# Reordering the gates, copies and banks around four stages of a two-layer SSM and MLP gradient kernel

## The chip, the cores and the metric

The kernel runs on one core of one Trainium2 chip. TensorE multiplies matrices into PSUM (eight banks of 128 partitions by 512 float32 values here), VectorE and ScalarE read PSUM and work element by element, GpSimd does small work and issues DMAs from its own queue, and SyncE (SP) issues most other DMAs. Each engine runs its own list of instructions in order and waits for the others through semaphores. The metric is the device time of one execution in microseconds; several executions are timed, and their median counts. One further execution was profiled, and all rows of the trace come from it.

## What is computed

The reference runs four residual layers forward and then takes the gradient of everything (a vector-Jacobian product with `grad_out`):

```python
x = A_q
x = x + A(layernorm(x))     # H3: q * (long_conv(short_conv(k) * v) + ...)
x = x + B(layernorm(x))     # MLP: silu(h @ w1) @ w2
x = x + A(layernorm(x))     # the same weights again
x = x + B(layernorm(x))
```

There are 2048 rows of 448 channels; the MLP is 1792 wide. In A, `k` is convolved with a four-tap kernel, multiplied by `v`, and convolved with a kernel as long as the sequence through an FFT of length 4096. That result, Y, does not depend on x, so both A layers use the same Y, and `A(n) = n * Y`. The kernel returns the output and the gradients of q, k, v, the two convolution kernels, the skip vector, w1 and w2 (nine outputs; the gradient of w1 is output 7, that of w2 output 8).

## The kernel before, in words

**Prefix** (`_ssm_prefix`). The convolution as matrix products: a first FFT stage, a turn of 128x128 blocks, a second stage, the product of two spectra, and the inverse. `k_turn` transposes the long kernel, 128 channels at a time (16 TensorE transposes into one PSUM tile of two banks, then a copy of each half, one by VectorE and one by ScalarE, L406 and L116/L117). `k_stage1` multiplies the turned kernel by the FFT matrix (L420). All PSUM tiles of this part share one tag `A` with four buffers of two banks. `PRODUCTS` is an order written out by hand: `M` is the product of the spectra on VectorE (L573), `V` the second inverse stage on TensorE (L260, L261, function `_fft_inv_stage2_full`), `v` its copy out of PSUM by ScalarE (a) or VectorE (d). The list ends `... V9 v7a v9a`. The last inverse stage `ys()` (L604, copies L607) follows and needs all the copies.

**Main** (class `Main`, `run`). The rows are worked in four chunks c of 512 rows, four tiles of 128 rows each; L is 0 for the first pair of layers and 1 for the second. The steps of a chunk are generators, and `weave("OOLOOG...")` advances one of them per letter, which writes TensorE's order out by hand:
- `fwd0(c)`: layer norm of the input (`_ln`, statistics L309, the power on GpSimd L314, normalisation L317), then `gate` (L727 the product with Y as tile `a_t`, L728 the sum into `X`), then the statistics and the normalisation of the second layer norm, `n01`. `fwd0_end` holds the normalisation back until a sum of O has run. `fwd1` does the same for the second pair of layers. `x_load` fetches the input rows of a later chunk on SP's queue.
- `H` and, in chunk 0, `Hh` (halves of 256 rows): the pre-activations (`full` L681 and `rest` L685 into `ps_h`), SiLU by ScalarE (L816 in `Hh`, L833 in `H`), and a copy of the pre-activations into `Dall` (L116 ScalarE or L117 VectorE). `Hh` has four groups; those listed in `single` use two one-bank tiles of tag `po`, the others a two-bank tile of tag `mm`; those in `dv` are copied by VectorE.
- `O`: the second MLP product (L850, `ps_o`, tag `po`) and the sum into X on VectorE (L855). In the second pair of layers of chunks 1 to 3 the sums have high priority.
- `G`: the gradient of the activations (L681 and L685 into `ps_g`), copied into `ghT` (L116 or L117; `dv` names the pairs that VectorE copies) and multiplied by the slopes (L1013). `slope` is ScalarE's derivative of SiLU (L843).
- `N`: the gradient of the MLP input (L889) and the backward of layer norm and gate on VectorE (L905 to L917, L1063 to L1068).
- `T`, `transp_half`: turns of normalised rows on TensorE (L658, L669), copied to `nT`.

PSUM tags in this part: `mm` two buffers of two banks, `po` and `tr` two buffers of one bank each.

**Suffix** (`_ssm_suffix`, `Jobs`). The gradients of the convolution, with the weight gradients woven in as jobs (`ps_d` L1115, 16 row blocks each of two operands). `Jobs.last` makes the last 128 rows of w1's gradient in two halves of 224 columns; `flush` turns a finished block with TensorE (L1220) and stores it.

**What sets the order.** In the main part TensorE's order is the program's. VectorE, ScalarE, GpSimd and SP are ordered by a planner that walks the program with estimated durations and takes the earliest traced instruction that is ready, or one of high priority. `tc.issue_after(i)` puts the instructions of its block behind instruction i where they run on the same engine.

Of the kernel before, what the change touches and what calls it, by code (L numbers as in the profile page):

```python
# [254 lines left out]
def _fft_inv_stage2_full(k, pa, pb, ci, psum):  # L255
    nc = k.nc
    ga, gb = (G_IAF, G_IBF) if ci % 2 else (G_IA, G_IB)
    pv = psum.tile([P, 8, P], FP32, name="ps_v", **k.pt["v"])
    for i in range(8):
        nc.tensor.matmul(pv[:, i, :], lhsT=pa[:, i * P:(i + 1) * P], rhs=k.Gpre[:, ga, :], start=True, stop=False)  # L260
        nc.tensor.matmul(pv[:, i, :], lhsT=pb[:, i * P:(i + 1) * P], rhs=k.Gpre[:, gb, :], start=False, stop=True)  # L261
    return pv
# [80 lines left out]
def _ssm_prefix(k):  # L343
# [4 lines left out]
    with ExitStack() as es:  # L348
# [51 lines left out]
        def k_turn(lo, hi):  # L400
            n = hi - lo
            kview = ksb[lo // P][:n].rearrange("p (n1 n2) -> p n2 n1", n2=16)
            pt = psum.tile([P, 2, 1024], BF16, name="ps_kt", **a_)
            pv = pt[:, :, 0:8 * n].rearrange("p g (i d) -> p g i d", d=n)
            for i in range(16):
                nc.tensor.transpose(pv[:, i // 8, i % 8, :], kview[:, i, :], k.ident[:n, :n])  # L406
            for g, e in enumerate((nc.vector, nc.scalar)):
                last = _copy(nc, e, Kt[:, 8 * g:8 * g + 8, lo:hi], pv[:, g])
# [167 lines left out]
        def V(ci):  # L576
            pab = live["V", ci]
            live["v", ci] = _fft_inv_stage2_full(k, pab[:, 1], pab[:, 0], ci, psum)

        def v(ci, part, eng):  # L580
            _copy(nc, eng, B1[:, 8 * ci:8 * ci + 8, :].rearrange("p a b -> p (a b)"), live["v", ci][:].rearrange("p a b -> p (a b)"))
# [34 lines left out]
class Main:  # L616
# [101 lines left out]
    def a_fwd(self, c, si, src, n_g, groups):  # L718
        _ln(self.k, self.ch, c, src, si, n_g, groups)
        self.gate(c, src, n_g)  # L720

# [19 lines left out]
    def fwd0(self, c):  # L741
# [187 lines left out]
    def run(self, ys):  # L929
# [47 lines left out]
        hs = [self.Hh(0, 1, nT, aT, dT2, 0, (1, 3), (1,)), self.Hh(0, 1, nT, aT, dT2, 1)]  # L977
# [4 lines left out]
        self.transp_half(self.n1[1], nT, GBLK, 1)  # L982
# [3 lines left out]
        for c in range(4):  # L986
# [8 lines left out]
            if c < 2:  # L995
# [477 lines left out]
```

## Time and profile before

| | us |
|---|---|
| median of 3 executions | 688.93 (688.62 to 689.18) |
| the profiled execution, its own time | 687.9 |
| its span, first to last instruction | 686.1 |
| TensorE busy | 665.3 (97%) |
| VectorE busy | 482.2 (70%) |
| ScalarE busy | 429.7 (63%) |
| GpSimd busy | 104.6 (15%) |

The granted TensorE clock is 0.999 of full speed over the span. In a timeline row stand the start, the duration, the engine, the line, the operation, output and input, the shape and the count; a bracket gives how long the engine idled before it and what ended that. "Who waited for whom" rows give total time, number of times and the longest. In rows of stretches the columns are the length, then busy time and count of TensorE, its weight loads, VectorE, ScalarE and GpSimd, then the granted clock, the DMA engines' busy share and GB/s. The prefix runs to about 84 us, chunk 0 starts there, the backward steps of chunk 0 at 154, those of chunks 1 and 2 near 246 and 338, and the suffix ends the span. Matmul durations contain latency and overlap, so the pitch of matmuls is taken from rows of many.

### The profile page before, as it was taken

The page shows a single profiled execution, that of the slowest core. Times are in us where ns is not written, and L with a number is a line of the kernel's source. Part 1 is how long each engine was busy: PE and PEld are TensorE (multiplying, and loading weights), DVE is VectorE, ACT ScalarE, POOL GpSimd, SP SyncE. Part 2 cuts the span into 40 slices and gives each one's busy share as a digit, 9 for nine tenths or more (in the row PEclk, how much of TensorE's full clock was granted, in tenths as well). Part 3 has the DMA queues.
Part 4 walks back from the last instruction along what each step waited for, and adds up shares of the span by engine and source line. Part 5 has one row for each costly group of instructions (what it writes and reads, how often), then busy time and mean ns, then how long its engine had stood idle before and what let it go on. Part 6 is the DMA issues. An engine that isn't in the chain of part 4 may idle for free.

```text
span 686.1 us, 14467 instructions
## 1 busy us (share of the span) xinstructions
PE 665.3 (97%) x5844; PEld 362.3 (53%) x5879; DVE 482.2 (70%) x1133; ACT 429.7 (63%) x528; POOL 104.6 (15%) x177
## 2 busy tenths in 40 slices
PE   8989999999999899999899999999999999999997
PEld 6876755554444344444444444544555555555666
DVE  5779954677879858898588874843937554528992
ACT  5988987888758668678477685123634543653431
POOL 1047320110010100101001000010111211102311
PEclk9999999999999999999999999999999999999999
DMA  8999989499788767598776799859599988956981
GB/s 316 248 278 316 342 191 227 112 228 258 191 241 228 219 163 193 123 250 231 182 162 193 218 241 375 241 173 205 200 238 354 324 274 323 351 173 223 324 308 42
DMA packets 203956, 162.60 MB, mean 237 GB/s; under 512 B 153505, under 2 KB 184244, under 8 KB 203122
## 3 DMA queue, kind: packets, MB, share of 16 engines
q1 hardware_dynamic: 190806, 113.35, 61.7%
q0 software_dynamic: 11088, 39.84, 17.1%
q10 hardware_dynamic: 1996, 8.49, 3.8%
q8 instruction: 46, 0.75, 0.4%
q14 instruction: 20, 0.16, 0.1%
HBM read 66.05 MB, written 54.60 MB: 176 GB/s over the span
## 4 chain that ended last, share of the span: by engine, by line
PE 77%; DVE 11%; ACT 5%; DMA 3%; issue 2%; POOL 1%; DVEq 0%; POOLq 0%
PE ps_d L1115 25%; PE ps_n L889 11%; PE ps_o L850 9%; PE ps_g L681 9%; PE ps_h L681 7%; PE ps_v L272 2%; PE ps_g L685 2%; PE ps_h L685 2%; DMA spec_K<-KAB 2%; DVE ln_st L309 1%; ACT KAB L116 1%; DVE lb_v L1063 1%; DMA KAB<-KAB 1%; PE ps_gK L1398 1%; PE ps_y L604 1%
## 5 line engine op out<-in xcount | busy, mean ns | idle before, releaser
L1115 PEld LDWEIGHTS <-dstat 128*128 128x128 bf16 x928 | 87.1, 98 | 75.7 <-issue 4.0
L889 PE MATMUL ps_n<-w1T,ghT 128*128 128x448 bf16 x448 | 94.5, 353 | 0.0
L850 PE MATMUL ps_o<-w2sb,aT 128*128 128x448 bf16 x448 | 89.2, 353 | 1.8 <-DVE X L855 1.8
L116 ACT CAST ghT<-ps_g 128x1024 bf16<-128x1024 f32 (+1 forms) x54 | 48.3, 899 | 60.9 <-PE ps_g L685 46.8
L681 PE MATMUL ps_h<-nT,w1sb 128*128 128x512 bf16 (+1 forms) x410 | 83.0, 336 | 2.1 <-DVE Dall L117 0.8
L681 PE MATMUL ps_g<-nT,w2T 128*128 128x512 bf16 x317 | 77.9, 379 | 1.6 <-ACT Dall L116 0.4
L889 PEld LDWEIGHTS <-ghT 128*128 128x128 bf16 x448 | 42.4, 98 | 45.3 <-issue 4.7
L850 PEld LDWEIGHTS <-aT 128*128 128x128 bf16 x448 | 43.2, 98 | 41.8 <-issue 3.5
L681 PEld LDWEIGHTS <-w1sb 128*128 128x128 bf16 x420 | 39.1, 98 | 37.1 <-issue 8.2
L1063 DVE SCALAR_TENSOR_TENSOR lb_v<-lb_u,n 128x448 bf16<-128x448 bf16 x60 | 37.2, 621 | 27.6 <-ACT lb_u L905 27.2
L833 ACT ACTIVATE aT<-ps_h 128x1024 bf16<-128x1024 f32 (+1 forms) x48 | 44.2, 922 | 19.7 <-PE ps_h L681 11.5
L116 ACT CAST Dall<-ps_h 128x1024 bf16<-128x1024 f32 (+2 forms) x60 | 54.8, 913 | 0.0
L843 ACT ACTIVATE Dall<-Dall 128x1024 bf16<-128x1024 bf16 (+1 forms) x48 | 53.3, 1186 | 0.1
L681 PEld LDWEIGHTS <-w2T 128*128 128x128 bf16 x336 | 31.3, 98 | 40.9 <-issue 5.9
L314 POOL TENSOR_TENSOR rstd<-ln_ve,mhalf 128x2 f32<-128x2 f32 (+1 forms) x24 | 19.6, 818 | 183.7 <-DVE ln_ve L313 183.7
L1115 PE MATMUL ps_d<-X,dstat 128*128 128x448 bf16 x224 | 47.6, 353 | 0.0
L1115 PE MATMUL ps_d<-go,dstat 128*128 128x448 bf16 x224 | 47.2, 353 | 0.0
L1115 PE MATMUL ps_d<-n3m,dstat 128*128 128x448 bf16 (+1 forms) x240 | 47.0, 340 | 0.0
L1115 PE MATMUL ps_d<-n1m,dstat 128*128 128x448 bf16 (+1 forms) x240 | 46.5, 340 | 0.0
L116 ACT CAST A1g<-ps_v 128x1024 bf16<-128x1024 f32 x14 | 14.9, 1064 | 36.5 <-PE ps_v L272 36.5
L855 DVE TENSOR_TENSOR X<-X,ps_o 128x448 bf16<-128x448 bf16 x32 | 19.5, 611 | 18.4 <-PE ps_o L850 18.2
L905 ACT ACTIVATE lb_u<-ps_n,rstd 128x448 bf16<-128x448 f32 x32 | 20.5, 639 | 16.8 <-PE ps_n L889 13.0
(210 smaller groups left out, 1111.9 us busy)
## 6 DMA issues: line engine op xcount, KB each, us to landing
dstat<-a_d SPq DMA_DIRECT2D x28, 512.0 KB, 5.0
dstat<-g_d SPq DMA_DIRECT2D x28, 512.0 KB, 5.4
a_d<-turned SPq DMA_DIRECT2D x16, 512.0 KB, 3.0
g_d<-turned SPq DMA_DIRECT2D x16, 512.0 KB, 3.0
a_d<-turned SPq DMA_DIRECT2D x16, 384.0 KB, 2.7
g_d<-turned SPq DMA_DIRECT2D x16, 384.0 KB, 2.8
spec_K<-KAB POOLq DMA_DIRECT2D x7, 512.0 KB, 6.3
KAB<-KAB POOLq DMA_DIRECT2D x28, 128.0 KB, 5.1
```

The lines of the kernel that those rows point to most:

```text
L116: return nc.scalar.copy(out, in_)
L314: nc.gpsimd.tensor_tensor(out=r[:, lo:hi], in0=ve[:, lo:hi], in1=k.mhalf[:, lo:hi], op=ALU.pow)
L681: self.nc.tensor.matmul(ps, lhsT=w[:, b, ft * P:(ft + 1) * P], rhs=x[:, b], start=(start and b == 0), stop=(stop and b == bs[2]))
L685: self.nc.tensor.matmul(ps, lhsT=w[sl, b, ft * P:(ft + 1) * P], rhs=x[sl, b], start=start, stop=stop)
L833: self.last_silu = nc.scalar.activation(aT[hh][:, o:o + hi - lo, :], ps(lo, hi), ACT.Silu)
L843: self.nc.scalar.activation(dT[hh][:, o:o + n, :], dT[hh][:, o:o + n, :], ACT.Derivative_silu)
L850: nc.tensor.matmul(po[:, :D], lhsT=aT[ft // 7][:, ft % 7, tl * P:(tl + 1) * P], rhs=self.w2sb[:, ft, :], start=(ft == 0), stop=(ft == NF - 1))
L855: self.last_o = nc.vector.tensor_tensor(out=X[:, t, :], in0=X[:, t, :], in1=po[:, :D], op=ALU.add)
L889: nc.tensor.matmul(pns[tl][:, :D], lhsT=gh[h][:, ft % 7, tl * P:(tl + 1) * P], rhs=self.w1T[:, ft, :], start=(ft == 0), stop=(ft == NF - 1))
L905: nc.scalar.activation(u0[:], pn[:, :D], ACT.Identity, scale=k.rstd[2 * L + 1][:, t:t + 1], accum_out=cp[:, tl, 0:1])
L1063: nc.vector.scalar_tensor_tensor(out=v[:], in0=u0, scalar=-1.0 / D, in1=n_t, op0=ALU.mult, op1=ALU.mult, accum_out=cp[:, 1:2])
L1115: self.nc.tensor.matmul(ps[:, cols], lhsT=st[:, t, :], rhs=mov[:, t, cols], start=(first and t == 0), stop=(last and t == NT - 1))
```

## The change

Five edits.

1. `fwd0` for chunks 1 to 3 no longer runs the gates at once; they move to a first step of `fwd0_end`, with the statistics of the second layer norm. For c above 1 that step stands behind the last traced sum of O, which is that of the first output tile, since the weave has a letter L after `OO`. For the rows of chunk 1, prepared in chunk 0, the gates keep their place. `x_load` moves behind the gates. The normalisation is a second step (the second L).
2. `G` of the second pair of layers in chunks 1 and 2 has all its copies on ScalarE; before, pairs 1 and 4 were copied by VectorE. Chunk 3 is as it was.
3. In chunk 0, `Hh` of the first half takes the third group through single `po` banks instead of the second, VectorE copies the pre-activations of the second and third groups instead of the second and fourth, and the copy of the second half's turn goes to VectorE.
4. `k_turn` uses two one-bank tiles per turn, and the inverse product 9, the last of the list, two tiles of four blocks, whose copies go to ScalarE and VectorE.
5. `Jobs.last` makes the first 336 columns as one product and the last 112 columns already turned, with the roles of the two operands exchanged; VectorE copies them, and SP stores them.

```diff
-def _fft_inv_stage2_full(k, pa, pb, ci, psum):
+def _fft_inv_stage2_full(k, pa, pb, ci, psum, parts):
     ...
-    pv = psum.tile([P, 8, P], FP32, name="ps_v", **k.pt["v"])
+    n = 8 // parts
+    pvs = [psum.tile([P, n, P], FP32, name="ps_v", **k.pt["v"]) for _ in range(parts)]
     for i in range(8):
-        nc.tensor.matmul(pv[:, i, :], lhsT=pa[:, i * P:(i + 1) * P], ...)
+        pv = pvs[i // n]
+        nc.tensor.matmul(pv[:, i % n, :], lhsT=pa[:, i * P:(i + 1) * P], ...)
     ...
@@ k_turn
-            pt = psum.tile([P, 2, 1024], BF16, name="ps_kt", **a_)
-            pv = pt[:, :, 0:8 * n].rearrange("p g (i d) -> p g i d", d=n)
+            pv = []
+            for g in range(2):
+                pt = psum.tile([P, 1024], BF16, name="ps_kt", **a_)
+                pv.append(pt[:, 0:8 * n].rearrange("p (i d) -> p i d", d=n))
     ...
@@ V and v
-            live["v", ci] = _fft_inv_stage2_full(k, pab[:, 1], pab[:, 0], ci, psum)
+            live["v", ci] = _fft_inv_stage2_full(k, pab[:, 1], pab[:, 0], ci, psum, 2 if ci == 9 else 1)
 
         def v(ci, part, eng):
-            _copy(nc, eng, B1[:, 8 * ci:8 * ci + 8, :]..., live["v", ci][:]...)
+            pvs = live["v", ci]
+            n = 8 // len(pvs)
+            for e, i in zip((eng, nc.vector), range(len(pvs))):
+                _copy(nc, e, B1[:, 8 * ci + n * i:8 * ci + n * i + n, :]..., pvs[i][:]...)
@@ fwd0
-            self.a_fwd(c, 0, xc, n00, ((0, 4),))
+            _ln(k, self.ch, c, xc, 0, n00)
             self.n0[c] = (n00, n01)
-            norm = _ln_parts(k, self.ch, c, self.xs(c), 1, n01, ((0, 4),))
-            next(norm)
-            self.norm = self.fwd0_end(c, norm, n01)
+            self.norm = self.fwd0_end(c, xc, n00, n01)
     ...
-    def fwd0_end(self, c, norm, n01):
+    def fwd0_end(self, c, xc, n00, n01):
+        norm = _ln_parts(self.k, self.ch, c, self.xs(c), 1, n01, ((0, 4),))
+        with self.tc.issue_after(self.last_o.ins) if c > 1 else nullcontext():
+            self.gate(c, xc, n00)
+            next(norm)
+        if c < 3:
+            self.x_load(c + 1)
+        yield
         with self.tc.issue_after(self.last_o.ins):
-            next(norm, None)
+            next(norm)
@@ run
-        hs = [self.Hh(0, 0, nT, aT, dT1, 0, (1, 3), (1,)), self.Hh(0, 0, nT, aT, dT1, 1)]
+        hs = [self.Hh(0, 0, nT, aT, dT1, 0, (1, 2), (2,)), self.Hh(0, 0, nT, aT, dT1, 1)]
     ...
-            self.transp_half(self.n0[0][1], nT, GBLK, 1)
+            self.transp_half(self.n0[0][1], nT, GBLK, 1, nc.vector)
     ...
     # the same two edits for the second pair of layers of chunk 0
     ...
                 if c == 0:
                     next(self.norm)
-            if c < 2:
-                self.x_load(c + 2)
+                    next(self.norm)
     ...
-                g = self.G(gT, gh2, dv=(1, 4))
+                g = self.G(gT, gh2, dv=(1, 4) if c == 3 else ())
                 if c < 3:
-                    weave("OOLOOGOGOGOGGOGTG", O=o, G=g, L=self.norm, T=...)
+                    weave("OOLOOLGOGOGOGGOGTG", O=o, G=g, L=self.norm, T=...)
@@ Jobs.last
-        for h in range(2):
-            cols = slice(h * D // 2, (h + 1) * D // 2)
-            ps = self.bank(None)
-            for i in range(2):
-                for n, _ in enumerate(self.mms(ps, sts[i], movs[i](), 0, NT, i == 0, i == 1, cols)):
-                    if h + i == 1 and n == 2:
-                        self.flush()
+        cols = slice(0, 3 * DC)
+        ps = self.bank(None)
+        for i in range(2):
+            yield from self.mms(ps, sts[i], movs[i](), 0, NT, i == 0, i == 1, cols)
+        nc.scalar.copy(o[:, cols], ps[:, cols])
+        self.flush()
+        self.pend = (ft, o, 0, 3)
+        ps = self.bank(None)
+        for i in range(2):
+            for t in range(NT):
+                nc.tensor.matmul(ps[:DC, 0:P], lhsT=movs[i]()[:, t, 3 * DC:D], rhs=sts[i][:, t, :], ...)
+                if i == 1 and t == 3:
+                    self.flush()
+                if t % 8 == 7:
                     yield 1
-            nc.scalar.copy(o[:, cols], ps[:, cols])
-            if h == 0:
-                self.flush()
-            self.pend = (ft, o, 2 * h, 2 * h + 2)
+        o7 = k.do7[ft % 4]
+        nc.vector.tensor_copy(o7[:, 3], ps[:DC, 0:P])
+        out7v = k.outs[7].rearrange("(c p) f -> p c f", p=DC)
+        nc.sync.dma_start(out=out7v[:, 3, ft * P:(ft + 1) * P], in_=o7[:, 3])
```

More of the change, by code (lines that the diff above doesn't have):

```diff
@@ L252, in _fft_stage2_full @@
     return ps
[L255 removed]
+def _fft_inv_stage2_full(k, pa, pb, ci, psum, parts):
     nc = k.nc
     ga, gb = (G_IAF, G_IBF) if ci % 2 else (G_IA, G_IB)
[L258 removed]
+    n = 8 // parts
+    pvs = [psum.tile([P, n, P], FP32, name="ps_v", **k.pt["v"]) for _ in range(parts)]
     for i in range(8):
[L260 to L262 removed]
+        pv = pvs[i // n]
+        nc.tensor.matmul(pv[:, i % n, :], lhsT=pa[:, i * P:(i + 1) * P], rhs=k.Gpre[:, ga, :], start=True, stop=False)
+        nc.tensor.matmul(pv[:, i % n, :], lhsT=pb[:, i * P:(i + 1) * P], rhs=k.Gpre[:, gb, :], start=False, stop=True)
+    return pvs
 def _fft_inv_stage2_half(k, pa, pb, B1, ci, psum, cnd):
```

16 lines of the change are left out of this document (7 added, 9 removed).

## Prediction

> **What bounds the kernel now.** I read the page's busy shares first, then TensorE's list of waits, then the timelines around the longest of them, then the chain's last steps.
>
> ```profile
> span 686.1 us, 14467 instructions
> PE 665.3 (97%) x5844; PEld 362.3 (53%) x5879; DVE 482.2 (70%) x1133; ACT 429.7 (63%) x528; POOL 104.6 (15%) x177
> ```
>
> TensorE is busy for 665.3 of 686.1 us. The edits take no matmul work away, so all that they can win lies in the 20.8 us in which it idles, and behind its last matmul.
>
> ```profile
> PE ps_g L685 <- DVE ghT L117: 3.1, 2, 1.6
> PE ps_o L850 <- DVE X L855: 1.8, 2, 0.9
> ...
> PE ps_y L604 <- ACT A1kv L116: 0.5, 1, 0.5
> ```
>
> The two longest waits come twice each: once in chunk 1, once in chunk 2. Here is chunk 1, TensorE and then VectorE:
>
> ```profile
> 229.06 1.48 PE L850 MATMUL ps_o<-w2sb,aT 128*128 128x448 bf16 x7 [0.90 <-DVE X L855]
> ...
> 236.55 0.39 PE L685 MATMUL ps_g<-nT,w2T 64*128 64x512 bf16 x2 [1.55 <-DVE ghT L117]
> ...
> 243.96 0.63 PE L658 MATMUL ps_t<-ident,n 64*128 64x64 bf16 x32
> ```
>
> ```profile
> 221.56 0.62 DVE L727 TENSOR_TENSOR a_t<-n,Ysb 128x896 bf16<-128x896 bf16 x1
> ...
> 226.44 0.59 DVE L309 BATCH_NORM_STATS2 ln_st<-X 128x6 f32<-128x448 bf16 x1
> ...
> 228.39 0.62 DVE L855 TENSOR_TENSOR X<-X,ps_o 128x448 bf16<-128x448 bf16 x1
> ...
> 232.04 0.20 DVE L313 TENSOR_SCALAR ln_ve<-ln_mv 128x4 f32<-128x4 f32 x1
> 234.05 1.31 DVE L317 TENSOR_SCALAR n<-X,ln_mv,rstd 128x448 bf16<-128x448 bf16 x4 [1.81 <-POOL rstd L314]
> 235.28 1.22 DVE L117 CAST ghT<-ps_g 128x1024 bf16<-128x1024 f32 x1
> ```
>
> The third output tile waits for a `po` bank until the first output sum, X L855, has run at 228.39. VectorE had put the next rows' two gates (from 221.56) and two of their statistics (to 226.44) ahead of that sum. The second gap is at 236.55: pair 4 of G needs the `mm` buffer of pair 1, whose copy VectorE makes at 235.28, behind a normalisation that sat 1.81 us waiting for GpSimd's power.
>
> **Part 1, chunks 1 and 2: gates behind the first sum, G's copies on ScalarE.** Ahead of the sum stood two a_t, two X and two statistics, six operations at 0.53 us of pitch (0.62 less the overlap), 3.2 us. Behind it they free the sum to start near 228.39 - 3.2 = 225.2; what of the backward work fills in makes it 226.5 at worst. Needed is 228.1 (229.06 less the 0.90, less a hop). The 0.90 goes. Queued behind the moved gates are the other statistics, the power and the normalisation, but the total work on VectorE up to 232.04 is the same in another order, so I leave the power and the normalisation where they are; they end at 235.3 and their reader is the turn at 243.96, so there is room even after the gaps are gone.
>
> For the other gap, ScalarE has this:
>
> ```profile
> 224.53 6.64 ACT L843 ACTIVATE Dall<-Dall 128x1024 bf16<-128x1024 bf16 x6
> 231.07 0.99 ACT L116 CAST ghT<-ps_g 128x1024 bf16<-128x1024 f32 x1
> 234.82 1.01 ACT L116 CAST ghT<-ps_g 128x1024 bf16<-128x1024 f32 x1 [2.76 <-PE ps_g L685]
> ```
>
> After the slopes it copies pair 0 to 232.06 and then idles 2.76 us. Pair 1's copy fits there: 232.1 to 233.1. Without the 0.90, TensorE would ask for that buffer at 236.55 - 1.55 - 0.90 = 234.1. So the 1.55 goes too. The copy of pair 4, which also moves to ScalarE, adds about 1.0 us there and takes 1.2 off VectorE; TensorE's next reader of that bank comes several matmul groups later. Late next: pair 2 needs the buffer of pair 0, free at 232.06, and TensorE would be there at about 232.1. I charge 0.15 for that. Per chunk 0.90 + 1.55 - 0.15 = 2.3; two chunks, **4.6**. Bounds: 4.9 if nothing is late, 1.6 if only the 0.90 or half of the 1.55 goes.
>
> The loads of the next input rows on SP's queue now stand behind the later gates. Behind them in that queue are stores of turned activations and the load of gradient rows. The rows loaded are first read a chunk later, and the stores' buffers (five of tag T) are asked for only in the next H, behind the turn at 243.96. I cost this at nothing; it would cost once the gates came more than some 10 us later. In chunk 0 the gates keep their place.
>
> **Part 2, chunk 0: third group through single banks.**
>
> ```profile
> 102.04 0.81 PE L681 MATMUL ps_h<-nT,w1sb 128*128 128x256 bf16 x6 [0.61 <-ACT Dall L116]
> ...
> 125.87 1.48 PE L681 MATMUL ps_h<-nT,w1sb 128*128 128x256 bf16 x12
> ...
> 134.48 0.81 PE L681 MATMUL ps_h<-nT,w1sb 128*128 128x256 bf16 x6 [0.83 <-DVE Dall L117]
> ```
>
> ```profile
> 126.17 0.99 ACT L116 CAST ghT<-ps_g 128x1024 bf16<-128x1024 f32 x1
> ...
> 132.60 0.84 ACT L816 ACTIVATE aT<-ps_h 128x768 bf16<-128x768 f32 x1
> ```
>
> In layer 0 the second half's first group waits 0.61 for the third group's copy (ScalarE) in its `mm` buffer. Now that buffer holds the second group, read out by VectorE one group earlier, and the turned copy has left ScalarE: the 0.61 goes, **0.6**. In layer 1 the 0.83 is a wait for the fourth group, whose pre-activation copy follows its SiLU (132.60). There the order changes: the second group now needs the `mm` buffer of G's pair, which ScalarE copies only at 126.17 to 127.1. The group would start at about 126.5 (halfway through the row at 125.87), so a new wait of 0.6 arises. It is made up: what followed had 0.83 of wait, less 0.6 leaves **0.25**. Bounds for both together: 1.4 (no new wait), 0 (the new wait adds to a remaining one). The turned copies go to VectorE, which has nothing there for the single banks yet; the extra instruction of the split (four groups become two SiLUs and two copies in the third instead of the second) is a swap.
>
> **Part 3, the start.** Each K turn now fills two one-bank tiles.
>
> ```profile
> 5.36 2.20 PE L406 MATMUL ps_kt<-ident,ksd 128*128 128x128 bf16 x32
> 8.35 1.91 PE L420 MATMUL ps_s<-KAB,M1sb 128*128 128x256 bf16 x16 [0.78 <-DVE KAB L117]
> ...
> 13.05 3.46 PE L420 MATMUL ps_s<-KAB,M1sb 128*128 128x192 bf16 x32 [0.52 <-DVE KAB L117]
> ```
>
> ScalarE beside it, and the stretch that follows (columns as in the table's text):
>
> ```profile
> 7.28 2.06 ACT L116 COPY KAB<-ps_kt 128x1024 bf16<-128x1024 bf16 x2 [4.60 <-DVE KAB L117]
> ```
>
> ```profile
> 18.70:84.10 65.40, 60.32 (x963) 49.82 (x969) 56.52 (x78) 58.01 (x60) 29.02 (x54) 1.00 1.08 292
> ```
>
> The copies of a turn ran one after the other (ScalarE's first is released by VectorE's), and the first began only when all 16 transposes were done. With tiles of their own the first can start 8 transposes (0.55 us) earlier: 0.5 at 8.35 and 0.4 at 13.05, at most 0.9. Against it: two turns now take all four buffers of tag A. Then comes the stretch to 84.1, in which the DMA engines are full (share 1.08) and ScalarE works 58 of 65 us, so part is absorbed. I take **0.4**, between 0.9 and -0.3 (buffers short).
>
> **Part 4, the last inverse product.** Its copy is split over two engines.
>
> ```profile
> 83.00 1.01 ACT L116 CAST A1kv<-ps_v 128x1024 bf16<-128x1024 f32 x1 [0.63 <-PE ps_v L261]
> ```
>
> ```profile
> 81.86 1.23 DVE L117 CAST A1kv<-ps_v 128x1024 bf16<-128x1024 f32 x1
> ...
> 98.93 0.69 DVE L117 CAST Dall<-ps_h 128x512 bf16<-128x512 f32 x1 [4.32 <-ACT aT L816]
> ```
>
> TensorE waits 0.5 for ScalarE's 1024-wide copy. A 512-wide one takes VectorE 0.69; it can start when its copy from 81.86 ends at 83.09, so it ends at 83.7, against ScalarE's 84.0 before: **0.35**, from 0 to 0.5. The product's second buffer is one that an earlier copy has freed.
>
> **Part 5, the tail.** The chain's last steps, a row of TensorE's timeline, and a group of the page:
>
> ```profile
> 659.18 3.78 PE ps_d L1115 x20
> ...
> 680.14 1.93 PE ps_d L1115 x20
> ...
> 682.10 0.35 ACT dout L1130
> ...
> 682.49 0.33 PE ps_dt L1220 x2
> ...
> 682.85 0.29 DVE wts L117
> ```
>
> ```profile
> 18.67 3.73 PE L450 MATMUL ps_kT<-ident,k_n 128*112 128x128 bf16 x64
> ```
>
> ```profile
> L1115 PEld LDWEIGHTS <-dstat 128*128 128x128 bf16 x928 | 87.1, 98 | 75.7 <-issue 4.0
> ```
>
> Before: 64 matmuls of 224 columns at 1.93/20 = 96 ns, 6.2 us, then 1.07 us (682.07 to 683.14) of copy, transposes and copy. After: 32 of 336 columns at 143 ns (between 96 and 3.78/20 = 189) and 32 of 128 columns with a new weight each, at 3.73/64 = 58 ns: 4.6 + 1.9 = 6.5. Behind them stands only one VectorE copy, some 0.3. That is +0.3 and -0.75; SP must issue a second store right behind the first, which I charge 0.05: **0.4**, from 0.7 to -0.2.
>
> What could spoil this is the weight: a load of one takes 98 ns, more than the matmul, but the row at 18.67 shows that loads overlap. The Trainium skill, in "TensorE: Matmul & The Clock Gate", section "Back-to-back issue gap", gives about 81 ns per matmul for a sustained stream of load and matmul at 128 columns. This trace does not agree (58 ns, a new weight each time); by the page's figure the second part would take 32 x 81 ns = 2.6 us and the tail would lose 0.3 instead of winning 0.4, an estimate.
>
> **Sum.** 4.6 + 0.6 + 0.25 + 0.4 + 0.35 + 0.4 = 6.6 us. The profiled execution took 687.9 us, so its like would take 681.3. The median shown is 688.93, 1.0 above it, so I predict **682.3 us**.
>
> **Rivals.** First a row of chunk 1, in the order TensorE, its weight loads, VectorE:
>
> ```profile
> 204.00:232.00 28.00, 26.94 (x137) 12.12 (x139) 26.89 (x91) 25.39 (x31) 2.00 (x3) 1.00 0.84 225
> ```
>
> 1. *VectorE is the bound, and the gaps only move* (0.12). From 204 to 232 VectorE works 26.89 of 28 us, so a wait removed may come back behind L1013's products. Against it: each chunk takes 2.4 us of copies off VectorE. Then Part 1 gives nothing: 688.9 - 2.0 = 686.9.
> 2. *One of the two gaps stays* (0.12): the planner still lists the sum late, or ScalarE's copy of pair 1 late. 688.9 - 4.3 = 684.6.
> 3. *Slower: the gates come too late for the turn* (0.06). Gates, statistics, power and normalisation take about 4 x 0.53 + 4 x 0.6 + 1.8 (232.24 to 234.05) + 1.3 = 7.6 us in a row; the turn, moved up to 241.5, needs them. If the planner puts the gates behind the products at 240 or so, the turn starts at 248, 6.5 late per chunk: 682.3 + 13 = 695. The kernel becomes slower than before once the gates start 11.5 us or more behind the first sum (8.2 of slack and half of 6.6). Against it: VectorE idles 1.81 and more before that, and takes what is ready.
> 4. *The tail is paced by weight loads* (0.03): 32 x 98 ns instead of 32 x 58, +1.3: 683.6. The page named above stands on this side.
> 5. *Gains given back in small new waits elsewhere*, about no change (0.03).
>
> **Numbers.** The forecast has the remaining 0.64, by itself 680.8 to 684.3 from the bounds of the small terms. The range reaches up into the first rival: 680.6 to 687.0. A measurement of this kernel tells 0.2% (1.4 us) from no change. Faster: 0.64 + 0.12 + 0.03 and most of rival 1, 0.88; same 0.06; slower 0.06.
>
> **What would show it.** Right: in chunks 1 and 2 no TensorE wait on X L855 or on ghT L117, the first sum ahead of L727, ghT copies of pairs 1 and 4 on ScalarE; the 0.61 gone; in layer 1 a wait of ps_h on ScalarE's ghT copy instead of the 0.83; ps_y released some 0.3 earlier; one copy behind the last matmul. Wrong: ps_t L658 waiting on n, a wait on VectorE at L1013's readers, or ps_y no earlier than 84 although the first ps_s is.

## The result, and the profile after

| | before | after |
|---|---|---|
| median | 688.62 (687.87 to 689.18, 5 executions) | 681.62 (680.6 to 682.5, 5 executions) |
| profiled execution, its own time | 687.9 | 680.6 |
| its span | 686.1 | 678.8 |

The ratio is 0.9901 (95% interval 0.9887 to 0.9914): 1% faster, 7.0 us, where 6.6 us and 682.3 were forecast. Lines have moved: X's sum L855 is now L863, the output product L850 is L858, the gates L727 and L728 are L730 and L731, G's products L681 and L685 are L688 and L692, the turn L658 is L665, the gradient product L889 is L897.

The page of after, busy times:

```profile
span 678.8 us, 14462 instructions
PE 665.2 (98%) x5843; PEld 361.5 (53%) x5878; DVE 481.2 (71%) x1132; ACT 430.9 (63%) x529; POOL 104.4 (15%) x177
```

TensorE is as busy as before, to 0.1 us; its idle time fell from 20.8 to 13.6 us. All of the gain was idle time, as the prediction had it. Its list of waits (total, times, longest) no longer has the sum of X nor VectorE's copy of `ghT`. The new wait that was forecast is there, on ScalarE's copy of `ghT`, and `ps_y` now waits 0.3 for VectorE's half copy instead of 0.5 for ScalarE's whole one:

```profile
PE ps_w L398 <- DVE zero L395: 1.2, 1, 1.2
...
PE ps_h L688 <- ACT ghT L116: 0.5, 1, 0.5
...
PE ps_y L611 <- DVE A1kv L117: 0.3, 1, 0.3
```

**Chunk 1.** TensorE's timeline, before, at the two ends of the stretch (first output product, first gradient product):

```profile
220.87 5.46 PE L850 MATMUL ps_o<-w2sb,aT 128*128 128x448 bf16 x28
...
245.82 1.49 PE L889 MATMUL ps_n<-w1T,ghT 128*128 128x448 bf16 x7
```

and after:

```profile
219.05 5.46 PE L858 MATMUL ps_o<-w2sb,aT 128*128 128x448 bf16 x28
...
226.39 1.48 PE L858 MATMUL ps_o<-w2sb,aT 128*128 128x448 bf16 x7
...
231.72 0.82 PE L692 MATMUL ps_g<-nT,w2T 64*128 64x512 bf16 x6
...
239.55 0.63 PE L665 MATMUL ps_t<-ident,n 64*128 64x64 bf16 x32
...
241.42 1.49 PE L897 MATMUL ps_n<-w1T,ghT 128*128 128x448 bf16 x7
```

Between these two ends the only idle time is 0.16 us of issue at 240.34, ahead of five of G's products, which before has too (at 244.75); the six short products at 231.72 run in one piece, where four and two stood with 1.55 us between them. The stretch takes 241.42 - 219.05 = 22.37 us, 2.58 less than before's 24.95. VectorE of after in the same stretch, then ScalarE:

```profile
225.72 0.61 DVE L863 TENSOR_TENSOR X<-X,ps_o 128x448 bf16<-128x448 bf16 x1
226.25 1.15 DVE L730 TENSOR_TENSOR a_t<-n,Ysb 128x896 bf16<-128x896 bf16 x2
...
232.82 1.31 DVE L319 TENSOR_SCALAR n<-X,ln_mv,rstd 128x448 bf16<-128x448 bf16 x4 [1.15 <-POOL rstd L316]
```

```profile
229.26 1.90 ACT L116 CAST ghT<-ps_g 128x1024 bf16<-128x1024 f32 x2
...
236.59 1.01 ACT L116 CAST ghT<-ps_g 128x1024 bf16<-128x1024 f32 x1 [0.71 <-PE ps_g L688]
```

The sum stands ahead of the gates, and ScalarE copies pairs 0 and 1 behind each other from 229.26.

**Chunk 0.** First output products of the two layers, before and after, and the new wait of after (TensorE's timeline):

```profile
103.78 1.49 PE L850 MATMUL ps_o<-w2sb,aT 128*128 128x448 bf16 x7
...
136.22 1.49 PE L850 MATMUL ps_o<-w2sb,aT 128*128 128x448 bf16 x7
```

```profile
102.48 1.49 PE L858 MATMUL ps_o<-w2sb,aT 128*128 128x448 bf16 x7
...
125.91 0.81 PE L688 MATMUL ps_h<-nT,w1sb 128*128 128x256 bf16 x6 [0.52 <-ACT ghT L116]
...
134.40 1.49 PE L858 MATMUL ps_o<-w2sb,aT 128*128 128x448 bf16 x7
```

**The last inverse product and the tail.** The two half copies of `ps_v` run side by side, and the chain of after ends with one copy (the chain's columns are start, length, engine, output, line):

```profile
81.55 1.83 DVE L117 CAST A1kv<-ps_v 128x1024 bf16<-128x1024 f32 x2
82.24 0.58 ACT L116 CAST A1kv<-ps_v 128x512 bf16<-128x512 f32 x1 [0.19 <-PE ps_v L263]
...
83.52 1.68 PE L611 MATMUL ps_y<-A1kv,Minvsb 128*128 128x448 bf16 x8 [0.30 <-DVE A1kv L117]
```

```profile
669.58 2.96 PE ps_d L1122 x20
...
674.50 0.69 PE ps_d L1139 x12
675.18 0.02 issue
675.21 0.29 DVE wts L1145
```

**Where the time went.** Each column is the way between the starts of two rows of TensorE's timeline: the first key turn `ps_kT`, the last inverse stage `ps_y`, the first output product of chunk 0 in each layer, its first gradient product `ps_n`; in chunks 1 and 2 from the first output product to the first gradient product; and from the first turn of a weight gradient (`ps_dt`) to the span's end. The experiments stand in it for the next section.

| kernel | kT starts | kT to y | y to O, layer 0 | O to O, layer 1 | O to N | chunk 1 | chunk 2 | dt to end |
|---|---|---|---|---|---|---|---|---|
| before | 18.67 | 65.39 | 19.72 | 32.44 | 17.56 | 24.95 | 24.95 | 102.03 |
| after | 18.34 | 65.18 | 18.96 | 31.92 | 17.56 | 22.37 | 22.38 | 101.69 |
| e1_gates | 18.61 | 65.39 | 19.86 | 32.44 | 17.56 | 26.92 | 27.23 | 101.99 |
| e2_copies | 20.17 | 65.52 | 19.72 | 32.44 | 17.56 | 23.23 | 23.23 | 102.09 |
| e3_chunk0 | 18.56 | 65.39 | 18.95 | 31.93 | 17.55 | 24.96 | 24.96 | 101.97 |
| e4_ends | 19.43 | 65.18 | 19.72 | 32.44 | 17.55 | 24.96 | 24.95 | 101.68 |
| e5_gates_copies | 19.10 | 65.41 | 19.72 | 32.44 | 17.56 | 22.36 | 22.35 | 102.08 |
| e6_chunk0_gates | 18.25 | 65.26 | 20.44 | 31.93 | 26.06 | 22.36 | 22.36 | 101.68 |
| e7_second_in_po | 18.10 | 65.17 | 18.95 | 32.41 | 17.56 | 22.36 | 22.36 | 101.68 |
| e8_third_sum | 18.24 | 65.19 | 18.95 | 31.93 | 17.56 | 23.81 | 23.81 | 101.74 |
| e9_load_behind | 19.46 | 65.15 | 18.96 | 31.58 | 17.56 | 22.36 | 22.37 | 101.74 |
| e10_after_again | 18.61 | 65.19 | 18.95 | 31.93 | 17.56 | 22.38 | 22.37 | 101.70 |

From before to after: 0.33 + 0.21 + 0.76 + 0.52 + 2.58 + 2.57 + 0.34 = 7.3 us, the whole difference of the spans. Where the code of a way is the same, it repeats to some 0.15 us from one execution to the next (the exception is e6's 20.44, where the products of `ps_y` waited 1.4 us for one of ScalarE's copies in that execution). The start scatters by 2 us. The ways that the table leaves out are 67.0 to 67.1 us each between a gradient product and the next chunk's output product, and 246.3 us from the last gradient product in the table to the first `ps_dt`, before and after.

### The profile page after: what moved, and what is told of

Read it like the earlier page. It is cut to its first block, busy times and chain, and to the rows that moved or that the text cites. A ratio compares the mean times of both kernels' runs of the same rounds, so it can differ in the third digit from the quotient of the medians.

```text
span 678.8 us, 14462 instructions
## 1 busy us (share of the span) xinstructions
PE 665.2 (98%) x5843; PEld 361.5 (53%) x5878; DVE 481.2 (71%) x1132; ACT 430.9 (63%) x529; POOL 104.4 (15%) x177
## 4 chain that ended last, share of the span: by engine, by line
PE 84%; DVE 5%; ACT 4%; DMA 3%; issue 2%; POOL 1%; DVEq 0%; POOLq 0%; ACTq 0%
PE ps_d L1122 25%; PE ps_n L897 12%; PE ps_o L858 11%; PE ps_g L688 10%; PE ps_h L688 9%; PE ps_v L274 2%; PE ps_g L692 2%; PE ps_h L692 2%; DMA spec_K<-KAB 2%; ACT KAB L116 1%; PE ps_gK L1412 1%; PE ps_y L611 1%; ACT Dall L851 1%; PE ps_gkv L1383 1%; PE ps_s L225 1%
## 5 line engine op out<-in xcount | busy, mean ns | idle before, releaser
L1122 PEld LDWEIGHTS <-dstat 128*128 128x128 bf16 x896 | 84.2, 98 | 76.9 <-issue 4.0
L897 PE MATMUL ps_n<-w1T,ghT 128*128 128x448 bf16 x448 | 94.4, 353 | 0.0
L858 PE MATMUL ps_o<-w2sb,aT 128*128 128x448 bf16 x448 | 89.2, 353 | 0.1
L116 ACT CAST ghT<-ps_g 128x1024 bf16<-128x1024 f32 (+1 forms) x58 | 52.2, 907 | 51.8 <-PE ps_g L692 38.5
L688 PE MATMUL ps_h<-nT,w1sb 128*128 128x512 bf16 (+1 forms) x410 | 83.0, 336 | 1.1 <-ACT ghT L116 0.5
L688 PE MATMUL ps_g<-nT,w2T 128*128 128x512 bf16 x317 | 77.9, 379 | 1.6 <-ACT Dall L116 0.4
L897 PEld LDWEIGHTS <-ghT 128*128 128x128 bf16 x448 | 42.4, 98 | 45.3 <-issue 4.7
L858 PEld LDWEIGHTS <-aT 128*128 128x128 bf16 x448 | 43.2, 98 | 40.5 <-issue 2.1
L688 PEld LDWEIGHTS <-w1sb 128*128 128x128 bf16 x420 | 39.1, 98 | 36.2 <-issue 7.3
L841 ACT ACTIVATE aT<-ps_h 128x1024 bf16<-128x1024 f32 (+1 forms) x48 | 44.2, 922 | 19.7 <-PE ps_h L688 11.5
L688 PEld LDWEIGHTS <-w2T 128*128 128x128 bf16 x336 | 31.3, 98 | 40.9 <-issue 5.9
L863 DVE TENSOR_TENSOR X<-X,ps_o 128x448 bf16<-128x448 bf16 x32 | 19.5, 612 | 23.1 <-PE ps_o L858 23.1
```

What stands on the lines that cost most here:

```text
L116: return nc.scalar.copy(out, in_)
L688: self.nc.tensor.matmul(ps, lhsT=w[:, b, ft * P:(ft + 1) * P], rhs=x[:, b], start=(start and b == 0), stop=(stop and b == bs[2]))
L841: self.last_silu = nc.scalar.activation(aT[hh][:, o:o + hi - lo, :], ps(lo, hi), ACT.Silu)
L858: nc.tensor.matmul(po[:, :D], lhsT=aT[ft // 7][:, ft % 7, tl * P:(tl + 1) * P], rhs=self.w2sb[:, ft, :], start=(ft == 0), stop=(ft == NF - 1))
L863: self.last_o = nc.vector.tensor_tensor(out=X[:, t, :], in0=X[:, t, :], in1=po[:, :D], op=ALU.add)
L897: nc.tensor.matmul(pns[tl][:, :D], lhsT=gh[h][:, ft % 7, tl * P:(tl + 1) * P], rhs=self.w1T[:, ft, :], start=(ft == 0), stop=(ft == NF - 1))
```

## The experiments

The theory is the prediction's own sum: each edit takes away the waits named there and brings its term alone as well as beside the others. The rivals are that an edit alone only moves its gap, that the gates may stand anywhere without cost, and that the new wait in chunk 0 eats what the reordering wins. First the edits one by one, each put alone into the kernel before.

### e1_gates: the gates alone

```diff
-                    weave("OOLOOGOGOGOGGOGTG", O=o, G=g, L=self.norm, T=...)
+                    weave("OOLOOLGOGOGOGGOGTG", O=o, G=g, L=self.norm, T=...)
# with fwd0, fwd0_end and the second next(self.norm) as in the change
```

> The kernel before with the gates of chunks 2 and 3's rows moved behind the first output sum (and the input loads behind them) and nothing else. Theory (each TensorE wait has its own cause): the 0.90 us wait on X L855 goes in both chunks, the 1.55 us wait on VectorE's ghT copy of pair 1 stays or grows, since the copy still stands behind the normalisation on VectorE: about 1.8 us faster, 686.8. Rival (VectorE is the bound and the wait only moves): the wait on ghT grows by 0.9 and the time stays at 688.6.

Measured: 692.24 us, ratio 1.0041 (1.0024 to 1.0058). Slower: both expectations are missed in time, on the far side, though both had the wait on the copy growing. TensorE in chunk 1, then VectorE (in this kernel L855 is the output product):

```profile
237.22 0.61 PE L685 MATMUL ps_g<-nT,w2T 64*128 64x512 bf16 x2 [2.99 <-DVE ghT L117]
237.77 2.65 PE L855 MATMUL ps_o<-w2sb,aT 128*128 128x448 bf16 x7
```

```profile
234.72 1.32 DVE L317 TENSOR_SCALAR n<-X,ln_mv,rstd 128x448 bf16<-128x448 bf16 x4 [1.14 <-POOL rstd L314]
235.96 1.22 DVE L117 CAST ghT<-ps_g 128x1024 bf16<-128x1024 f32 x1
```

The 0.90 is gone, as it should be. But TensorE now reaches pair 4 earlier and VectorE's copy of pair 1 runs later, 235.96 against 235.28: it stands behind the normalisation, and the normalisation behind the gates. So 0.90 + 1.55 = 2.45 us of idle became 2.99. That alone would be 0.5 us per chunk. The rest is the second row: seven products of 448 columns take 2.65 us, where they take 1.49 elsewhere. Rows of stretches around it (columns as explained under "Time and profile before"), the one before the gap's end, the one behind it, and the next:

```profile
234.00:236.50 2.50, 0.23 (x4) 0.00 (x0) 1.78 (x5) 1.01 (x1) 0.85 (x2) 1.00 0.35 95
236.75:240.00 3.25, 2.78 (x9) 0.98 (x9) 2.18 (x3) 0.00 (x0) 0.18 (x1) 0.50 0.44 161
240.25:243.00 2.75, 2.70 (x13) 1.27 (x13) 0.96 (x1) 1.17 (x2) 0.00 (x0) 1.00 0.62 141
```

Behind the gap the granted clock is 0.50 for about 3.4 us (in quarter-microsecond stretches from 236.7 to 240.1), of which TensorE works 2.9 and so loses about 1.45. Sum for chunk 1: -2.45 + 2.99 + 1.45 = +2.0; the table shows 26.92 - 24.95 = 1.97. Chunk 2 has the same 2.99 and a stretch at 0.50 from 332.3 to 335.7: +2.28. The timed executions say the same: their mean clock is 0.999 in one (689.77 us), 0.997 in four (690.86 to 692.75) and 0.995 in two (692.24 and 693.69), and 3.4 us at half clock are 0.0025 of 690 us, which fits none, one and two such stretches. Read so, a gap of 3 us sometimes halves the clock and sometimes does not; only one of these executions, with two stretches, was profiled.

### e2_copies: G's copies alone

```diff
-                g = self.G(gT, gh2, dv=(1, 4))
+                g = self.G(gT, gh2, dv=(1, 4) if c == 3 else ())
```

> The kernel before with G's copies of pairs 1 and 4 on ScalarE in chunks 1 and 2 and nothing else. Theory: the 1.55 us wait goes in both chunks and the 0.90 us wait on X L855 stays: about 3.1 us faster, 685.5. Rival (VectorE is the bound): the waits move behind the products of L1013 and the time stays at 688.6.

Measured: 685.28 us, ratio 0.9954 (0.9942 to 0.9967), as expected.

```profile
230.71 1.49 PE L850 MATMUL ps_o<-w2sb,aT 128*128 128x448 bf16 x7 [0.91 <-DVE X L855]
...
236.04 0.82 PE L685 MATMUL ps_g<-nT,w2T 64*128 64x512 bf16 x6
```

The wait for the sum stays, the wait for the copy is gone, and 1.72 us per chunk are won. This part stands without the other; the other does not stand without this one.

### e3_chunk0: the order of chunk 0 alone

```diff
-        hs = [self.Hh(0, 0, nT, aT, dT1, 0, (1, 3), (1,)), self.Hh(0, 0, nT, aT, dT1, 1)]
+        hs = [self.Hh(0, 0, nT, aT, dT1, 0, (1, 2), (2,)), self.Hh(0, 0, nT, aT, dT1, 1)]
# the same for dT2, and the second half's turns copied by nc.vector
```

> The kernel before with only chunk 0's edits (third group in single banks, copies of the second and third groups and of the turn on VectorE). Theory: the step from the first pre-activations to the first O product is 0.76 us shorter, and the stretch from the second layer's first group to its first O product 0.5 us shorter, with a new wait of 0.5 us on ScalarE's ghT copy: 1.3 us faster in all, 687.3. Rival (the sum of parts hides an interaction): less than 0.8.

Measured: 687.54 us, ratio 0.9985 (0.9973 to 0.9997): 1.0 us faster by the ratio, 1.5 by the median of before on the same chip (689.02), and so as expected. The table shows 0.77 and 0.51 us, the same two amounts as in the kernel after: this part is independent of the others.

### e4_ends: both ends alone

```diff
-            pt = psum.tile([P, 2, 1024], BF16, name="ps_kt", **a_)
+            for g in range(2):
+                pt = psum.tile([P, 1024], BF16, name="ps_kt", **a_)
# with V, v, _fft_inv_stage2_full and Jobs.last as in the change
```

> The kernel before with only the turns, the split last inverse product and the new last weight gradient. Theory: the kT transposes start 0.3 to 0.9 us earlier than 18.67, the y product 0.2 earlier still, and the end after the last matmul is 0.3 to 0.4 us shorter: 0.9 to 1.6 us faster, 687.0 to 687.7. If the slow first transposes of the changed kernel's profile (16 in 1.1 to 1.3 us more than before) belong to the edit, they show here again; if they are a matter of that execution, the kT transposes start near 17.8.

Measured: 688.4 us, ratio 0.999 (0.9975 to 1.0005): no difference that can be told, under what was expected. The table shows 0.21 us up to `ps_y` and 0.35 at the end, and a start that was 0.76 later in this execution. There TensorE waited 1.47 us for loads (0.42 for `M1sb`, 0.84 and 0.21 for `K_sb`), of which the profile of before has nothing, and the first 32 transposes took 2.57 us. So the start of this run decides neither side of the expectation; why the transposes are slow is settled in the last section.

### e5_gates_copies: both edits of Part 1

```diff
# e1_gates and e2_copies together
```

> The kernel before with both edits of chunks 1 and 2 (gates and copies) and nothing else. Theory (additive): neither wait is left and the time is 5.1 us shorter, 683.5. If one of the two edits alone had given nothing, this shows whether it takes both.

Measured: 684.01 us, ratio 0.9926 (0.9908 to 0.9944), as expected: 2.59 us per chunk. With the copy on ScalarE the 2.99 us gap of e1 does not arise, and the clock stays at 1.00. The gates' move is worth -2.0 to -2.3 us per chunk alone and +0.87 on top of the copies; the two are no sum.

### e6_chunk0_gates: the gates behind the sum in chunk 0 too

The kernel after, with the exception for chunk 0 taken away.

```diff
-        with self.tc.issue_after(self.last_o.ins) if c > 1 else nullcontext():
+        with self.tc.issue_after(self.last_o.ins) if c > 0 else nullcontext():
```

> The changed kernel with the gates of chunk 1's rows, too, behind the last traced output sum (in chunk 0 that is the second tile's). Theory (the chain of gates, statistics, power and normalisation takes 7.6 us and the turn needs it): the sum ends at 145.0, the chain at 152.6, the turn is due at 148.7, so TensorE waits 3.9 us there and the kernel takes 685.5. Rival (the planner or the slack absorbs it): 681.6.

Measured: 689.33 us, ratio 1.001 (0.9998 to 1.0022), 7.7 us above the kernel after: the side of the expectation that saw a stall, with twice its price. The chain from the gates to the end of the normalisation took 9.4 us (146.48 to 155.91) where 7.6 was counted; two of VectorE's products with the slopes (L1020) stand in it. TensorE's timeline, then two rows of stretches:

```profile
155.05 1.79 PE L665 MATMUL ps_t<-ident,n 64*128 64x64 bf16 x32 [4.77 <-DVE n L319]
156.78 5.33 PE L858 MATMUL ps_o<-w2sb,aT 128*128 128x448 bf16 x14
```

```profile
152.00:155.00 3.00, 0.00 (x0) 0.00 (x0) 2.08 (x5) 2.98 (x4) 1.66 (x1) 1.00 1.06 386
155.25:161.75 6.50, 6.28 (x46) 3.02 (x45) 3.86 (x7) 1.03 (x1) 0.60 (x1) 0.50 1.18 269
```

The turn waits 4.77 us for the normalisation, and then TensorE runs at half clock for 6.8 us (155.08 to 161.91), which costs another 3.4. The way from O to N grows by 8.5. Here the exception of the change carries as much as all its other parts.

### e7_second_in_po: the second group through single banks in layer 1

The kernel after; in layer 1 of chunk 0 the second group goes back to the single banks.

```diff
-        hs = [self.Hh(0, 1, nT, aT, dT2, 0, (1, 2), (2,)), self.Hh(0, 1, nT, aT, dT2, 1)]
+        hs = [self.Hh(0, 1, nT, aT, dT2, 0, (1, 2), (1,)), self.Hh(0, 1, nT, aT, dT2, 1)]
```

> The changed kernel with the second group, not the third, in single banks in the second pair of layers of chunk 0 (VectorE still copies the second and third groups). Theory: the 0.52 us wait on ScalarE's ghT copy goes, a wait of about 0.1 may come where the next G pair asks for the third group's buffer, and the kernel takes 681.2. Rival: the wait of 0.8 for the fourth group's buffer comes back and it takes 681.6 to 682.

Measured: 681.96 us, ratio 0.9896 (0.988 to 0.9913), no difference from after that can be told. The 0.52 is gone, and a longer wait comes 5 us later, where the theory had 0.1; the time is the rival's:

```profile
131.16 1.47 PE L688 MATMUL ps_g<-nT,w2T 128*128 128x512 bf16 x5 [0.68 <-DVE Dall L117]
```

The way between the output products is 32.41, 0.49 more than after. Of this, 0.16 is the longer wait; most of the rest comes from the turn of the second half (`ps_t` L676), which takes 0.87 us here and 0.61 in the kernel after. The kernel after accepts the shorter wait for the removal of this one.

### e8_third_sum: the gates behind the third sum

The kernel after, with the gates' letter later in the order of chunks 1 and 2.

```diff
-                    weave("OOLOOLGOGOGOGGOGTG", O=o, G=g, L=self.norm, T=...)
+                    weave("OOOOGOGOLLGOGGOGTG", O=o, G=g, L=self.norm, T=...)
```

> The changed kernel with the gates of chunks 2 and 3's rows behind the third output sum instead of the first, and the normalisation right behind. Theory (the slack of the chain towards the turn is 8.2 us): the third tile's product is done at about 230.4, its sum at 231.1, the chain at 238.7, and the turn is due at 239.55, so nothing is lost: 681.6. Rival (less slack, because the products of the slopes stand in the same list): the turn waits 1 us or more in each chunk, 684 and more.

Measured: 684.68 us, ratio 0.9937 (0.9916 to 0.9958): the rival. TensorE and VectorE in chunk 1:

```profile
240.05 1.47 PE L665 MATMUL ps_t<-ident,n 64*128 64x64 bf16 x32 [0.44 <-DVE n L319]
```

```profile
232.24 0.61 DVE L863 TENSOR_TENSOR X<-X,ps_o 128x448 bf16<-128x448 bf16 x1
232.76 1.16 DVE L730 TENSOR_TENSOR a_t<-n,Ysb 128x896 bf16<-128x896 bf16 x2
...
239.60 1.31 DVE L319 TENSOR_SCALAR n<-X,ln_mv,rstd 128x448 bf16<-128x448 bf16 x4 [1.14 <-POOL rstd L316]
```

The gates start 6.5 us later than in the kernel after; the turn waits 0.44 and then takes 1.47 instead of 0.63, tile by tile behind the normalisation: 1.44 us per chunk. The products with the slopes do stand in the chain, as the rival had it: one (L1020) from 231.09 ahead of the third sum, one at 237.24 ahead of the power.

### e9_load_behind and e10_after_again: what holds the new wait

What releases the 0.52 of chunk 0 is a copy that ScalarE begins at 124.87, although its products ended at 123.4: between them ScalarE loads the SiLU table. e9 puts the load behind the copy; e10 is the kernel after, unchanged, on the same chip.

```diff
-        with tc.issue_after(self.transp_half(self.n1[1], nT, GBLK, 0).ins):
-            nc.scalar.activation(k.warm[:], k.mhalf[:], ACT.Silu)
-        go(g, hs[0], hs[0], hs[0])
+        self.transp_half(self.n1[1], nT, GBLK, 0), go(g)
+        with tc.issue_after(self.last_gc.ins): nc.scalar.activation(k.warm[:], k.mhalf[:], ACT.Silu)
+        go(hs[0], hs[0], hs[0])
# in G: self.last_gc = _copy(...)
```

> The kernel after, with one swap on ScalarE: in layer 1 of chunk 0 the load of the SiLU table and its warm-up (1.28 + 0.20 us at 123.46) come behind the copy of G's last pair instead of ahead of it. Theory (the wait of 0.52 us of the second group at 125.91 is only that copy, held up by the table load): the copy runs at 123.5, the second group follows the first without idle, the way from layer 0's first output product to layer 1's falls from 31.92 to about 31.3, and the time is 0.5 to 0.6 us below that of the kernel after. Rival (the first SiLU, now some 0.2 us later, holds up a later group): the wait comes back at the fourth group or in the second half, the way stays at 31.7 to 31.9, and the time is the same.

> The kernel after once more, unchanged, on the same chip as the run beside it: 681.6 within 0.7 us, the way from layer 0's first output product to layer 1's 31.92 again; what differs between its profile and the first one of this kernel lies ahead of the first turned keys (18.34 us there).

Measured: e9 681.24 us, ratio 0.9882 (0.9868 to 0.9895); e10 681.7 us, ratio 0.989 (0.9875 to 0.9905). The times don't separate the two; the traces do. TensorE and ScalarE of e9:

```profile
125.66 1.48 PE L688 MATMUL ps_h<-nT,w1sb 128*128 128x256 bf16 x12
```

```profile
124.52 1.01 ACT L116 CAST ghT<-ps_g 128x1024 bf16<-128x1024 f32 x1
125.55 1.28 ACT L988 ACT_TABLE_LOAD   x1
126.84 0.20 ACT L988 ACTIVATE warm<-mhalf 128x4 f32<-128x4 f32 x1
```

The second group follows the first without idle, and the way between the output products is 31.58 against 31.93 in e10. Of the 0.52, 0.35 is kept, less than expected. At the place of the wait 0.68 us are won (124.58 to 127.07, in the kernel after 123.49 to 126.66), but 0.33 are lost behind it, most of it at the turn of the second half: it starts at 129.54, ahead of the end of the normalisation that it reads (129.79), and takes 0.87 us instead of 0.61. e10 repeats every way of the table from the first turn on within 0.02 us; its profile is 1.1 us longer than that of after, and not only by the start, as expected: 0.3 lie there, and 0.6 are a wait of a weight gradient's product for a load (`dstat`) that the first profile does not have.

## Why the prediction was right

The median came out 0.7 us below the forecast, inside its own range and in the main for its own reasons; where a term came out by something else, this is said. By its steps:

- **Part 1**, 4.6 forecast, 5.15 measured. Both waits went, in both chunks. The first sum did not come to 225.2 to 226.5: it starts 6.67 us behind the first output product, 227.5 on before's clock (which is 220.87 - 219.05 = 1.82 us later in this chunk), since VectorE filled the place with backward work. It was still ahead of the 228.1 at which it was needed. The charge of 0.15 for pair 2 was not due: its products follow without idle. And a gap is not worth just its idle time: e2 takes away 1.55 and wins 1.72, e5 takes away another 0.91 and wins 0.87. One sentence was wrong in its form: the two gaps were priced as independent. e1 shows that without the copies the gates' move loses. The sum held only since both edits were made; the prediction's lower bound for this part, 1.6, would have missed e1 altogether.
- **Part 2**, 0.6 + 0.25 forecast, 0.76 + 0.52 measured. The 0.61 wait went. In layer 1 the new wait was forecast at 0.6 for ScalarE's `ghT` copy and measured at 0.52 in that place; the old 0.83 went. These two are worth 0.16 together: 0.85 won where the old wait stood (131.87 to 134.48, after 130.91 to 132.67), 0.69 lost at the new one (after 123.49 to 126.66, before 124.80 to 127.28). That the second term came out twice as large is luck: the other 0.34 is one that the prediction does not name, most of it at the turn of the second half, before and then after:

```profile
129.76 0.87 PE L669 MATMUL ps_t<-ident,n 128*128 128x128 bf16 x8
```

```profile
129.06 0.61 PE L676 MATMUL ps_t<-ident,n 128*128 128x128 bf16 x8
```

  In before it starts ahead of the end of the normalisation that it reads (130.00), in after behind it (128.71). e7 shows that the exchange was worth making, and e9 that the new wait lies in the order of a table load and that the turn takes back half of it.
- **Part 3**, 0.4 forecast, 0.33 in these two profiles. The list of waits of TensorE in the stretch from 3 to 20 us has, before and then after:

```profile
PE ps_s L420 <- DVE KAB L117: 1.3, 2, 0.8
```

```profile
PE ps_s L424 <- DVE KAB L117: 0.3, 1, 0.3
```

  So a full microsecond of waiting went, more than the 0.9 forecast as the most. The wait of 0.52 us ahead of the products behind the second turn stands in all five profiles with the old `k_turn` and in none of the seven with the new one. Counted from the end of the first 32 transposes, `ps_kT` starts 11.11 us later in before (7.56 to 18.67) and 10.18 later in after (8.16 to 18.34; 10.16 in e8, and 10.40 in e7 with 0.24 of waiting for a load): the term is worth 0.93 where no load is late, twice the forecast, and none of it was absorbed on the way to `ps_y`. That the two profiles show 0.33 is luck, since the products and transposes at the start took 0.60 us longer in that of after (last section). The start itself is too scattered to show it: 18.56 to 20.17 with the old `k_turn`, 18.10 to 19.46 with the new one.
- **Part 4**, 0.35 forecast, 0.21 measured (65.15 to 65.26 from turn to `ps_y` in the kernels with the edit, 65.39 to 65.52 in the others). VectorE's half copy ends at 81.55 + 1.83 = 83.38, which is the forecast 83.7 on a clock 0.33 earlier. The term failed by what follows: TensorE starts 0.14 behind this copy, at 83.52, and had started 0.05 behind ScalarE's (83.00 + 1.01 to 84.06).
- **Part 5**, 0.4 forecast, 0.34 measured. The terms: 148 ns per product of 336 columns (2.96 us for 20, forecast 143) and 58 ns per product of 128 columns with a new weight each (0.69 us for the last 12, forecast 58). The Trainium skill, "TensorE: Matmul & The Clock Gate", section "Back-to-back issue gap", has about 81 ns for such a stream; this trace does not agree, and the tail's loss that would follow from it did not come.
- **SP's loads behind the gates**, forecast at nothing: nothing of them appears in TensorE's waits.
- **Rivals.** 1 (VectorE is the bound) and 2 (one gap stays) are out for the change as a whole: no wait came back behind VectorE's products, and no gap stayed. Without the copies, in e1, the wait did come back on VectorE, at its copy of `ghT`. 4 (the tail is paced by weight loads) is out by the 58 ns, 5 (gains given back elsewhere) by the table. Rival 3 (the gates come too late for the turn) did not happen in the change, and e6 and e8 show it as a real mechanism with a nearer edge than forecast. In the kernel after the normalisation ends at 232.82 + 1.31 = 234.1 and the turn starts at 239.55: 5.4 us of slack, not 8.2. The step that failed is the gates' start: they begin at 226.25, on before's clock 228.1 (1.82 later), and the slack counted from 225.7 (241.5 - 7.6 - 8.2); the chain from them takes 7.9 us (226.25 to 234.1) where 7.6 was forecast. The turn came as forecast, 239.55 + 1.82 = 241.4. e8 starts the gates 6.5 us later and pays 1.44 per chunk. Adding what is missing to 3.5 per chunk, the whole gain would be lost when the gates start some 9 us behind the first sum, an estimate, and earlier if the clock falls; the prediction said 11.5.

## What to carry to other kernels

Before moving work ahead or back on an engine, list what else that engine still owes the bottleneck: the gates' move alone lost 3.2 us, since the next copy in VectorE's list became the wait, and won 0.87 us per chunk once that copy had gone elsewhere. Price an idle gap of TensorE of up to 1.55 us by its length: taking one away won between 0.04 us less (0.91 gave 0.87) and 0.17 more (1.55 gave 1.72), unless the next wait was hidden behind it (e9: 0.52 gave 0.35). The gaps of 2.99 and 4.77 us cost 1.4 to 3.7 us more than they changed in length, for the half clock behind them. Where times scatter by a microsecond, the ways between the same rows of two traces, which repeat to 0.15 us here, show terms of 0.2 us that the times don't.

## What the runs showed of the hardware

**The clock steps on a grid of 3.413 us and falls behind a step with enough idle time.** Gaps of up to 1.55 us left the granted clock at 1.00 in every profile. Both gaps of 2.99 us in e1's profile were followed by 3.4 us at 0.50, and the gap of 4.77 us in e6 by 6.8 us, twice as long; in e6 all timed executions have a mean clock of 0.993 to 0.995. In chunk 2 of e1 the fall came 1.1 us after TensorE had begun to work again (332.29, work from 331.17).

The times of the falls say why. Those of e1's profile, at 236.72, 332.29 and, behind the last work, 690.69, lie 28 and 105 times 3.413 us apart; those of e6's, at 155.08 and 690.97, 157 times. Cut each of the twelve profiles into steps of this length, counted back from its last fall. The clock was halved behind all 15 steps in which TensorE idled for 1.91 us or more by the rows of stretches (twelve of them at the end of a span) and behind none of the others, which idle for 1.55 at most. In e1 the steps ahead of the falls hold 2.48 and 2.28 us of the two gaps. A gap of 2.99 us that a point of the grid cuts in half would stay below 1.55 on both sides, which fits the executions of e1 without a fall; this is inferred, since none of them was profiled. Why the half clock lasted two steps in e6 and one in e1 is open. Open, too, are the mean clocks of 0.996 to 0.998 in 5 of the 54 executions of before that were timed beside the experiments, in 2 of e2's 10 and in 1 of e4's 10, which took 0.8 to 3.1 us longer than their medians: the profiles of these kernels hold no gap above 1.55 us.

The Trainium skill, "TensorE: Matmul & The Clock Gate", section "What's actually happening", has half the rate after an idle window of 3413 ns that runs freely, not from the start of the gap. The grid and its spacing agree with it; that the window has to be idle throughout does not, since 1.91 us of idle were enough here.

**The first products run at half the pace, though their rows say 1.00.** TensorE's timelines before and after:

```profile
1.19 4.34 PE L396 MATMUL ps_w<-zero 128*128 128x512 bf16 x10 [1.19 <-DVE zero L393]
```

```profile
5.43 2.73 PE L410 MATMUL ps_kt<-ident,ksd 128*128 128x128 bf16 x32
```

A warming product of 512 columns takes 0.43 us here, where six of that width take 1.46 us elsewhere, 0.24 each; the stretch from 3 to 5 us has a granted clock of 1.00. The 32 transposes behind them took 2.20 us before and 2.73 after, and 2.18 to 2.65 in the experiments whose keys came in time, with either `k_turn`. The grid of the falls explains the difference. Its first point with a whole step of the span ahead of it is at 3.91 us in e5, 4.19 in e3, 4.36 in e10, 4.61 in e1, 4.89 in e6 and 5.29 in before; in this order the ten warming products take 3.66, 3.80, 3.88, 4.01, 4.14 and 4.34 us. In the other six the point is at 5.51 (e2), 5.70 (e7), 6.10 (e9), 6.41 (e4), 6.60 (e8) and 6.80 (after), behind the warming products, which all take 4.45 us, and the transposes take 2.19, 2.28, 2.43, 2.57, 2.65 and 2.73. In e1, e3 and e10 the transposes take 2.28, 2.51 and 2.35 although the point lies ahead of them; this is left open. So the pace doubles at a point of the grid, and where that point falls belongs to the execution and not to `k_turn`.
